# Thirty heads of a decode step as ten turns of a hardware loop, with each head's weights stored behind its keys

## The chip, the cores and the metric

The kernel runs on one core of one Trainium2 chip. The core has five engines with an instruction stream each: TensorE (PE, matmul), VectorE (DVE), ScalarE (ACT), GpSimd (POOL) and SyncE (SP); here SP issues nearly all DMA transfers. They meet only through semaphores. The metric is device time of one execution in microseconds (us), from the start to the end of the program. Lower is better.

## The reference

One token goes through a transformer block: attention over a cache of 8192 positions in 32 heads of 192 channels, then a squared-ReLU feed-forward network, both with a layer norm that is scaled and shifted by a condition `c`. All data is float32. The caches are 201 MB each, 403 MB together, and each number in them is used once.

```python
mod = (_silu(c) @ w_mod).reshape(c.shape[0], 6, 1, -1)
sa, ca, ga, sb, cb, gb = (mod[:, i] for i in range(6))
h = _layernorm(x) * (1 + ca) + sa
q = (h @ wq).reshape(1, 1, 32, 192).transpose(0, 2, 1, 3)
scores = einsum("bhqd,bhkd->bhqk", q, k_cache) * 192 ** -0.5
o = einsum("bhqk,bhkd->bhqd", softmax(scores), v_cache)
x = x + ga * (o.transpose(0, 2, 1, 3).reshape(1, 1, 32 * 192) @ wo)
h = _layernorm(x) * (1 + cb) + sb
r = relu(h @ w1 + b1)
x = x + gb * ((r * r) @ w2 + b2)
```

## The kernel before

The cache of a head is laid out as 128 partitions of 64 positions, so a head's keys are one tile of 128 x 12288 numbers (6144 KB), and its values are another. Three such tiles fit in on-chip memory: the pool `strm` hands out three slots in turn (`slot`, L47). The stream of loads is k0, v0, k1, v1 and so on, and load n takes the slot that load n-3 had. All of it is issued by SP in program order (`load`, L148). A load of keys so waits until the values of two heads earlier in the stream have been used by TensorE; a load of values waits until VectorE and ScalarE have finished with the keys of the head before.

For each head (loop at L257, unrolled by Python, so that the built program holds 32 copies of the body):

- `keys` (L183): VectorE multiplies the keys by the query in four chunks of 16 positions (L190) and sums most of the products of a chunk (L192). ScalarE sums the other 23 of a partition's 64 positions (L195).
- `softmax` (L208): the maximum over a partition (L210), over all partitions by a matmul (L212) and VectorE (L214), then the exponential on ScalarE (L218) and its sum by a matmul with ones (`total`, L88). The reciprocal of that sum (`inverse`, L206) is done in the middle of the next head.
- `values` (L222): 32 matmuls in four column groups multiply probabilities and values into `ps_o` (L229). The profile shows each float32 matmul as two.

Heads are paired for the weights. `load_w` (L136) fetches wo of pair i and wq of pair i+1 as one transfer of 1920 KB for two heads, into tiles of their own. In the third chunk of a head `between` runs either `project` (L232) for the pair that is finished, where VectorE scales two heads' outputs (L236), TensorE turns them (L241), VectorE copies (L244) and TensorE multiplies by wo (L248); or `query` (L172), which makes the queries of the next pair on TensorE (L176) and ScalarE (L178). Even heads from 2 on carry the projection, odd heads the query.

Ahead of the heads stand the matmuls for the condition (`mod`, L121) and the first layer norm. Behind them come the projection of the last pair, the second layer norm and the feed-forward network; its weights `w1` and `gw2` go into the slots that come free (L277 to L284). The order of the work is the order in which it is written (`manual_schedule`, L45); semaphores are placed by the language where data or buffers need them.

Of the kernel before, what the change touches and what calls it, by code (L numbers as in the profile page):

```python
# [8 lines left out]
F32 = mybir.dt.float32  # L9
AF = mybir.ActivationFunctionType  # L10
# [3 lines left out]
P = 128  # L14
D = 640
# [10 lines left out]
NPAIR = H // 2  # L26
NPOS = SK // P
I = 16
NCH = NPOS // I
N_ACT = (7, 6, 6, 4)  # L30
TAIL_PARTS = 4
WO = 3 * D
WQ = KB * PW
W2_CUT = ((0, 6), (6, 5), (11, 1))
EPS = 1e-5


@with_exitstack
def block_kernel(ctx: ExitStack, tc: tile.TileContext, xc, kc, vc, wq0, wx, wo15, wm0, wm1, w1, gw2, bb, out):
    nc = tc.nc  # L40
    const = ctx.enter_context(tc.tile_pool(name="const", bufs=1))
    strm = ctx.enter_context(tc.tile_pool(name="strm", bufs=3))
    work = ctx.enter_context(tc.tile_pool(name="work", bufs=2))
# [3 lines left out]
    def slot(name):  # L47
        return strm.tile([P, NPOS * DH], F32, tag="slot", name=name, bufs=3)

# [3 lines left out]
    ones = const.tile([P, P], F32, name="ones")  # L53
    nc.vector.memset(ones, 1.0)

# [14 lines left out]

    def columns(src, n, name, pool=const, **how):

        t = pool.tile([P, n // 32, 32], F32, name=name, **how)
        nc.vector.transpose(t.rearrange("p b r -> p (b r)"), src)
        return t
# [9 lines left out]
    def total(src, name):  # L85

        ps = psum.tile([P, 512], F32, tag="sm", name="ps_" + name, bufs=2)
        nc.tensor.matmul(ps[:, :1], ones, src, start=True, stop=True)  # L88
        return ps[:, :1]

    def layernorm(x, copies, scale1, shift, name):
# [5 lines left out]
        nc.vector.tensor_scalar(m, total(s, name + "_tm"), 1.0 / (copies * D), None, op0=ALU.mult)  # L97
# [6 lines left out]
        nc.scalar.activation(sd, total(ss, name + "_tv"), AF.Sqrt, bias=eps_t, scale=1.0 / (copies * D))  # L104
# [16 lines left out]
    def mod(first, n, w):  # L121

        ps = psum.tile([P, 512], F32, tag="q", name=f"ps_mod{first}", bufs=2)
        for b in range(KB):
            wb = w[:, b].rearrange("p (m n) -> p m n", m=n)
            for g in range(G):
                nc.tensor.matmul(ps[32 * g:32 * (g + 1), :n * DG], e[:, b:b + 1].to_broadcast([P, 32]),  # L127
                                 wb[:, :, DG * g:DG * (g + 1)], start=(b == 0), stop=(b == KB - 1))
        nc.vector.tensor_copy(mods[:, first:first + n], ps[:, :n * DG].rearrange("p (m n) -> p m n", m=n))  # L129

    wm0_t = slot("wm0_t")
    nc.sync.dma_start(wm0_t[:, :KB * 2 * D], wm0)

    qb_t, w_t = {}, {}

    def load_w(i):  # L136

        w_t[i] = strm.tile([P, WO + WQ], F32, tag="w", name=f"w{i}", bufs=2)
        if i < 0:
            nc.sync.dma_start(w_t[i][:, WO:], wq0)  # L140
        elif i + 1 == NPAIR:
            nc.sync.dma_start(w_t[i][:, :WO], wo15)
        else:
            nc.sync.dma_start(w_t[i], wx[i])

    k_t, v_t = {}, {}

    def load(src, to, h, what):  # L148
        to[h] = slot(f"{what}{h}")
        n = TAIL_PARTS if h == H - 1 and what == "v" else 1  # L150
        w = NPOS * DH // n
        for c in range(n):
            nc.sync.dma_start(to[h][:, c * w:(c + 1) * w],
                              src[h].rearrange("(p i) d -> p (i d)", p=P)[:, c * w:(c + 1) * w])

    load_w(-1)
    wm1_t = slot("wm1_t")
    nc.sync.dma_start(wm1_t[:, :KB * 3 * D], wm1)
    load(kc, k_t, 0, "k")
    mod(0, 2, wm0_t[:, :KB * 2 * D].rearrange("p (b n) -> p b n", b=KB))  # L160
# [11 lines left out]
    def query(i):  # L172
        w = w_t[i - 1][:, WO:].rearrange("p (b n) -> p b n", b=KB)
        ps = psum.tile([P, 512], F32, tag="q", name=f"ps_q{i}", bufs=2)
        for b in range(KB):
            nc.tensor.matmul(ps[:, :PW], hR[:, b], w[:, b], start=(b == 0), stop=(b == KB - 1))  # L176
        qb_t[i] = work.tile([P, PW], F32, name=f"qb{i}", tag="qb")
        nc.scalar.activation(qb_t[i], ps[:, :PW], AF.Copy, scale=DH ** -0.5)  # L178

    att = psum.tile([P, 512], F32, tag="att", name="att")  # L180
    query(0)

    def keys(h, between):  # L183

        q = qb_t[h // 2][:, DH * (h % 2):DH * (h % 2 + 1)]
        sc = work.tile([P, NPOS], F32, tag="sc", name=f"sc{h}")
        t = k_t.pop(h).rearrange("p (i d) -> p i d", d=DH)
        for c in range(NCH):
# [4 lines left out]
            for i in range(n, I):  # L193
                jk = work.tile([P, DH], F32, tag="jk", name=f"jk{h}_{c}_{i}", bufs=2)
# [5 lines left out]
        return sc  # L200

    ri_t, ps_t, sum_t = {}, {}, {}

    def inverse(h):
        ri_t[h] = work.tile([P, 1], F32, tag="ri", name=f"ri{h}", bufs=3)
        nc.vector.reciprocal(ri_t[h], sum_t.pop(h))  # L206

    def softmax(h, sc):  # L208
        mp = work.tile([P, 1], F32, tag="mp", name=f"mp{h}")
        nc.vector.tensor_reduce(mp, sc, axis=AX.X, op=ALU.max)  # L210
        ps = psum.tile([P, 512], F32, tag="sm", name=f"ps_mx{h}", bufs=2)
        nc.tensor.matmul(ps[:, :P], mp.to_broadcast([P, P]), ident, start=True, stop=True)  # L212
        nm = work.tile([P, 1], F32, tag="nm", name=f"nm{h}")
        nc.vector.tensor_reduce(nm, ps[:, :P], axis=AX.X, op=ALU.max, negate=True)  # L214

        p = work.tile([P, NPOS, 16], F32, tag="p", name=f"p{h}", bufs=1)
        sp = work.tile([P, 1], F32, tag="sp", name=f"sp{h}")
        nc.scalar.activation(p, sc[:, :, None].to_broadcast([P, NPOS, 16]), AF.Exp, bias=nm, accum_out=sp)  # L218
        sum_t[h] = total(sp, f"sum{h}")
        return p  # L220

    def values(h, p):  # L222

        t = v_t.pop(h)
        ps_t[h] = psum.tile([P, 512], F32, tag="o", name=f"ps_o{h}", bufs=3)
        n = NPOS // 2
        for j in range(n):
            g = j % G
            nc.tensor.matmul(ps_t[h][32 * g:32 * (g + 1), :PW], p[:, 2 * j:2 * j + 2].rearrange("p e r -> p (e r)"),  # L229
                             t[:, PW * j:PW * (j + 1)], start=(j < G), stop=(j >= n - G))  # L230

    def project(i):  # L232
        os_ = work.tile([P, 2, PW], F32, tag="os", name=f"os{i}", bufs=1)
        for a in range(2):
            h = 2 * i + a
            nc.vector.tensor_scalar(os_[:, :, DH * a:DH * (a + 1)], ps_t.pop(h)[:, :PW].rearrange("p (e d) -> p e d", e=2),  # L236
                                    ri_t.pop(h), None, op0=ALU.mult)
        pt = psum.tile([P, 512], F32, tag="sm", name=f"ps_oT{i}", bufs=2)
        for j in range(3):
            for k in range(2):  # L240
                nc.tensor.matmul(pt[:, 32 * j:32 * (j + 1)], os_[:, k, P * j:P * (j + 1)], pick[:, k],  # L241
                                 start=(k == 0), stop=(k == 1))
        oT = work.tile([P, 96], F32, tag="oT", name=f"oT{i}")
        nc.vector.tensor_copy(oT, pt[:, :96])  # L244
        w = w_t.pop(i)[:, :WO].rearrange("p (j n) -> p j n", j=3)
        for j in range(3):
            for g in range(G):
                nc.tensor.matmul(att[32 * g:32 * (g + 1), :DG], oT[:, 32 * j:32 * (j + 1)],  # L248
                                 w[:, j, DG * g:DG * (g + 1)],
                                 start=(i == 0 and j == 0), stop=(i == NPAIR - 1 and j == 2))  # L250

    mod(2, 3, wm1_t[:, :KB * 3 * D].rearrange("p (b n) -> p b n", b=KB))
    cb1 = const.tile([P, DG], F32, name="cb1")
    nc.vector.tensor_scalar(cb1, mods[:, 4], 1.0, None, op0=ALU.add)
    x_t = spread(x_c, KB, "x_t")
    bbt = spread(bbc, FB + KB, "bbt")
    for h in range(H):  # L257
        i = h // 2
        if h and h < H - 1:
            load(kc, k_t, h, "k")  # L260
        if h == H - 2:
            load(kc, k_t, h + 1, "k")
        if h % 2 and h < H - 1 or h == H - 2:
            load_w(i)
        load(vc, v_t, h, "v")

        def between():
            if h % 2 == 0 and h:
                project(i - 1)
            elif h % 2 and i + 1 < NPAIR:  # L270
                query(i + 1)

        sc = keys(h, between)
        values(h, softmax(h, sc))


    w1_t = slot("w1_t")  # L277
    nc.sync.dma_start(w1_t[:, :KB * FF], w1)
    gw_t = slot("gw_t")
    a = 0  # L280
    for b0, n in W2_CUT:
        b = KB * D + (b0 + n) * D
        nc.sync.dma_start(gw_t[:, a:b], gw2[:, a:b])
        a = b  # L284
# [77 lines left out]
```

## Time and profile before

| what | value |
|---|---|
| two timed runs | 1074.88 and 1075.42 us, median 1075.15 us |
| profiled execution, span | 1072.6 us |
| instructions | 8839 |
| TensorE busy | 431.8 us (40%) |
| VectorE busy | 756.2 us (70%) |
| ScalarE busy | 320.1 us (30%) |
| read from memory | 451.82 MB, 421 GB/s over the span |
| packets of SP's DMA queue | 98.1% of 16 engines' span |

The span goes from the first to the last instruction of the program in the profiled execution. The profile states no other time for that execution; the two timed runs lie 2.3 and 2.8 us above its span. In the views of the profile a row begins with the line of the kernel and the engine (PEld is TensorE's weight load, SPq the part of SP that issues), then the operation and the tiles as output<-input. "Idle before" is how long the engine had nothing to do ahead of a group of instructions, with what ended it.

### The profile page before, as it was taken

How to read it: one execution, taken by the hardware profiler on the slowest of the kernel's cores; microseconds unless marked ns; L12 is line 12 of the kernel's file. 1: busy time of each engine (PE TensorE's matmuls, PEld its weight loads, DVE VectorE, ACT ScalarE, POOL GpSimd, SP SyncE). 2: the span in 40 equal slices, each digit the busy share in tenths (PEclk: the TensorE clock that was granted, in tenths of full speed). 3: DMA queues.
4: the chain of work that ended last, by engine and by line, in shares of the span. 5: the costliest groups of instructions: out<-in, count | busy, mean ns of one | idle time of the engine just before them, and what ended most of it. 6: DMA issues, size and time to landing. Idle time of an engine off the chain costs nothing.

```text
span 1072.6 us, 8839 instructions
## 1 busy us (share of the span) xinstructions
PE 431.8 (40%) x3176; PEld 205.0 (19%) x3176; DVE 756.2 (70%) x453; ACT 320.1 (30%) x1559; POOL 0.7 (0%) x6
## 2 busy tenths in 40 slices
PE   3243243435425353442436344242633434363246
PEld 1011121113112121211113122111312111131113
DVE  1675877858578685858868586885757778585872
ACT  1132332323233232323422233332322323232340
POOL 0000000000000000000000000000000000000000
PEclk8666566666656666575666656566665666666568
DMA  9999999999999999999999999999999999999976
GB/s 401 438 426 435 419 442 436 428 431 433 428 422 442 424 439 424 437 429 427 435 437 424 440 424 438 425 432 432 426 436 423 430 435 426 433 428 426 399 292 266
DMA packets 13299, 452.38 MB, mean 422 GB/s; under 512 B 1732, under 2 KB 1736, under 8 KB 2120
## 3 DMA queue, kind: packets, MB, share of 16 engines
q1 hardware_dynamic: 12968, 451.81, 98.1%
q8 instruction: 25, 0.41, 0.2%
q14 instruction: 18, 0.15, 0.0%
q10 hardware_dynamic: 288, 0.01, 0.0%
HBM read 451.82 MB, written 0.00 MB: 421 GB/s over the span
## 4 chain that ended last, share of the span: by engine, by line
DMA 41%; DVE 38%; PE 18%; ACT 2%; issue 1%; SPq 0%; DVEq 0%; ACTq 0%
DMA k<-in_kc 41%; DVE k L190 21%; DVE sc L192 14%; PE ps_o L229 11%; PE ps_oT L241 4%; ACT p L218 2%; PE ps_mx L212 1%; PE ps_sum L88 1%; DVE os L236 1%; DVE nm L214 0%; PE ps_f L299 0%; DVE oT L244 0%; DVE mp L210 0%; PE ps_y L315 0%; ACT L218 0%
## 5 line engine op out<-in xcount | busy, mean ns | idle before, releaser
L190 DVE TENSOR_TENSOR k<-k,qb 128x3072 f32<-128x3072 f32 x128 | 428.5, 3348 | 192.9 <-DMA k<-in_kc 192.9
L195 ACT ACTIVATE jk<-k 128x192 f32<-128x192 f32 x736 | 256.5, 349 | 614.5 <-DVE k L190 614.5
L192 DVE TENSOR_REDUCE sc<-k 128x10 f32<-128x1920 f32 (+2 forms) x128 | 282.0, 2203 | 4.4
L229 PE MATMUL ps_o<-v,p 128*32 128x384 f32 x2048 | 240.0, 638 | 2.2 <-DMA v<-in_vc 2.2
L241 PE MATMUL ps_oT<-pick,os 128*128 128x32 f32 x192 | 43.2, 395 | 266.1 <-DVE os L236 266.1
L212 PE MATMUL ps_mx<-ident,mp 128*128 128x128 f32 x64 | 25.4, 501 | 285.6 <-DVE mp L210 285.6
L195 ACT ACTIVATION_READ_ACCUMULATOR jk<-k 128x1 f32 x736 | 137.3, 186 | 0.0
L229 PEld LDWEIGHTS ps_o<-v,p 128*32 128x32 f32 x2048 | 75.6, 140 | 144.9 <-issue 142.2
L241 PEld LDWEIGHTS ps_oT<-pick,os 128*128 128x128 f32 x192 | 41.0, 321 | 277.3 <-DVE os L236 276.6
L212 PEld LDWEIGHTS ps_mx<-ident,mp 128*128 128x128 f32 x64 | 16.1, 311 | 304.8 <-DVE mp L210 273.7
L218 ACT ACTIVATE p<-sc,nm 128x1024 f32<-128x1024 f32 x32 | 36.7, 1147 | 80.9 <-DVE nm L214 80.8
L176 PE MATMUL ps_q<-w,hR 128*128 128x384 f32 x150 | 52.4, 496 | 0.1
L88 PE MATMUL ps_sum<-sp,ones 128*128 128x1 f32 x64 | 18.8, 363 | 56.5 <-ACT p L218 56.5
L176 PEld LDWEIGHTS ps_q<-w,hR 128*128 128x128 f32 x150 | 27.3, 190 | 25.5 <-issue 8.8
L248 PE MATMUL att<-w,oT 128*32 128x160 f32 x384 | 28.5, 464 | 5.6 <-DVE oT L244 5.6
L244 DVE COPY oT<-ps_oT 128x96 f32<-128x96 f32 x16 | 4.1, 258 | 36.2 <-PE ps_oT L241 36.2
L214 DVE TENSOR_REDUCE nm<-ps_mx 128x1 f32<-128x128 f32 x32 | 9.3, 292 | 28.5 <-PE ps_mx L212 28.5
L88 PEld LDWEIGHTS ps_sum<-sp,ones 128*128 128x128 f32 x64 | 16.1, 313 | 65.9 <-ACT p L218 65.9
L236 DVE TENSOR_SCALAR os<-ps_o,ri 128x384 f32<-128x384 f32 x32 | 18.2, 607 | 7.3 <-PE ps_o L229 7.3
L248 PEld LDWEIGHTS att<-w,oT 128*32 128x32 f32 x384 | 15.6, 162 | 11.9 <-DVE oT L244 7.7
L127 PE MATMUL ps_mod<-wm_t,silu 128*32 128x320 f32 (+1 forms) x80 | 9.3, 626 | 12.5 <-DVE silu L117 12.5
L129 DVE COPY mods<-ps_mod 128x320 f32<-128x320 f32 (+2 forms) x3 | 1.4, 479 | 15.4 <-PE ps_mod L127 15.4
(68 smaller groups left out, 76.5 us busy)
## 6 DMA issues: line engine op xcount, KB each, us to landing
k<-in_kc SPq DMA_DIRECT2D x32, 6144.0 KB, 29.0
v<-in_vc SPq DMA_DIRECT2D x31, 6144.0 KB, 25.7
w<-in_wx SPq DMA_DIRECT2D x15, 1920.0 KB, 34.3
v<-in_vc SPq DMA_DIRECT2D x4, 1536.0 KB, 15.8
wm_t<-in_wm SPq DMA_DIRECT2D x1, 4800.0 KB
w_t<-in_w SPq DMA_DIRECT2D x1, 3840.0 KB, 12.6
gw_t<-in_gw SPq DMA_DIRECT2D x1, 3520.0 KB, 20.5
wm_t<-in_wm SPq DMA_DIRECT2D x1, 3200.0 KB, 10.7
```

The costliest lines, as they stand in the source:

```text
L88: nc.tensor.matmul(ps[:, :1], ones, src, start=True, stop=True)
L127: nc.tensor.matmul(ps[32 * g:32 * (g + 1), :n * DG], e[:, b:b + 1].to_broadcast([P, 32]), wb[:, :, DG * g:DG * (g + 1)], start=(b == 0), s ...
L176: nc.tensor.matmul(ps[:, :PW], hR[:, b], w[:, b], start=(b == 0), stop=(b == KB - 1))
L190: nc.vector.tensor_mul(pr, pr, q[:, None, :].to_broadcast([P, I, DH]))
L192: nc.vector.tensor_reduce(sc[:, c * I:c * I + n], pr[:, :n], axis=AX.X, op=ALU.add)
L195: nc.scalar.activation(jk, pr[:, i], AF.Copy, accum_out=sc[:, c * I + i:c * I + i + 1])
L212: nc.tensor.matmul(ps[:, :P], mp.to_broadcast([P, P]), ident, start=True, stop=True)
L218: nc.scalar.activation(p, sc[:, :, None].to_broadcast([P, NPOS, 16]), AF.Exp, bias=nm, accum_out=sp)
L229: nc.tensor.matmul(ps_t[h][32 * g:32 * (g + 1), :PW], p[:, 2 * j:2 * j + 2].rearrange("p e r -> p (e r)"), t[:, PW * j:PW * (j + 1)], star ...
L236: nc.vector.tensor_scalar(os_[:, :, DH * a:DH * (a + 1)], ps_t.pop(h)[:, :PW].rearrange("p (e d) -> p e d", e=2), ri_t.pop(h), None, op0=A ...
L241: nc.tensor.matmul(pt[:, 32 * j:32 * (j + 1)], os_[:, k, P * j:P * (j + 1)], pick[:, k], start=(k == 0), stop=(k == 1))
L248: nc.tensor.matmul(att[32 * g:32 * (g + 1), :DG], oT[:, 32 * j:32 * (j + 1)], w[:, j, DG * g:DG * (g + 1)], start=(i == 0 and j == 0), sto ...
```

## The change

Heads 1 to 30 become a loop that the chip runs: `tc.For_i(1, 31, 3, iteration_sync="staggered")`, ten turns with three heads in the body. Heads 0 and 31 stand outside. The loop needs fixed buffers: three tiles `slot0` to `slot2`, three queries `qb`, three PSUM tiles `ps_o` and three reciprocals are allocated once, and the address of a load in memory comes from the loop's counter. The slots rotate as before.

All weights of a head now lie in memory behind its keys: a row of `kx` holds 12288 numbers of keys, 960 of wq for the next head and 960 of wo for the head before, 7104 KB for a head in one transfer. `project` and `query` work on one head each and both run in each head's third chunk. The reciprocal follows the sum at once, so on VectorE it stands ahead of the next head's keys. The weights for the last five vectors of the condition are loaded at the end (`wm1`, 6880 KB with wo of head 31), and the keys of head 31 come in two parts.

```diff
-    for h in range(H):
...
+    head(0, 0, 1, lambda: query(1, slots[0][:, KV:KV + HW]))
+
+    with tc.For_i(1, H - 1, NH, iteration_sync=SYNC) as i:
+        for r0 in range(NH):
+            r = (r0 + 1) % NH
+            ks, vs = (2 * r0 + 2) % 3, (2 * r0 + 3) % 3
+            load_k(i + r0, ks)
+            load_v(i + r0, vs)
+
+            def between():
+                project((r - 1) % NH, slots[ks][:, KV + HW:])
+                query((r + 1) % NH, slots[ks][:, KV:KV + HW])
+
+            head(r, ks, vs, between)
+
+    r = (H - 1) % NH
+    ks, vs = 2, 0
+    half = KV // 2
+    nc.sync.dma_start(slots[ks][:, :half], kx[H - 1, :, :half])
+    nc.sync.dma_start(slots[ks][:, half:KV + HW], kx[H - 1, :, half:KV + HW])
+    load_v(H - 1, vs)
+    head(r, ks, vs, lambda: project((r - 1) % NH, slots[ks][:, KV:KV + HW]))
+
+    M = KB * 4 * D
+    nc.sync.dma_start(slots[1][:, :M + HW], wm1)
...
+    def load_k(h, s):
+        nc.sync.dma_start(slots[s], kx[bass.ds(h, 1)].rearrange("o p n -> (o p) n"))
...
+    def project(r, w, last=False):
+        os_ = work.tile([P, 2, DH], F32, tag="os", name="os_", bufs=2)
+        nc.vector.tensor_scalar(os_, ps_o[r][:, :PW].rearrange("p (e d) -> p e d", e=2), rs_[r], None, op0=ALU.mult)
+        for k in range(2):
+            nc.tensor.matmul(ps_t[:, :32], os_[:, k, :P], pick[:, k], start=(k == 0), stop=(k == 1))
+        for k in range(2):
+            for a in range(2):
+                nc.tensor.matmul(ps_t[64 * a:64 * (a + 1), 32:64], os_[:, k, P:], pick[:, k],
+                                 start=(k == 0), stop=(k == 1))
...
-            if c == 0 and h:
-                inverse(h - 1)
...
+        nc.vector.reciprocal(rs_[r], total(sp))
```

The loop's semaphores have to be set back in each turn. With the staggered form the body is cut into four stages, 0 to 3, with a counter each (`sem_stage_0` to `sem_stage_3`). Each of the five engines counts itself in when it enters a stage. At the entry to a stage it first waits for its own results of two stages before, counts itself out of that stage, and then waits until that stage's counter is below one, which means that all five have counted themselves out. The entry to stage 0 stands at the turn's end, and there each engine counts itself out of stage 2.

On SP, this is how the loads of heads 1 to 3 stood before, with the semaphores that each waits for (DMAHW are landings of transfers; `_49` marks counters of the whole program):

```order
L153 DMA k2_412<-in_kc 128x12288 [waits DMAHW6_49,DMAHW2_49,PE_49]
L153 DMA v2_414<-in_vc 128x12288 [waits DMAHW3_49,DMAHW7_49,DVE_49,Activation_49]
L153 DMA k3_541<-in_kc 128x12288 [waits DMAHW1_49,PE_49]
L144 DMA w1_543<-in_wx 128x3840
L153 DMA v3_545<-in_vc 128x12288 [waits DMAHW2_49,DVE_49,Activation_49]
L153 DMA k4_656<-in_kc 128x12288 [waits DMAHW3_49,PE_49]
```

And this is the rest of a turn on SP now, from its third load on (`ISA` computes an address; `_stg0` marks counters that are set back in the loop):

```order
L137 DMA slot1_67<-in_kx 128x14208 [waits DMAHW4_49,PE_49]
L140 ISA [waits sem_stage_3_1186]
L140 DMA slot2_68<-in_vc 128x12288 [waits DMAHW0_I-283_stg0,DVE_I-283_stg0,Activation_I-283_stg0]
L137 ISA
L137 DMA slot0_66<-in_kx 128x14208 [waits PE_I-283_stg1,DMAHW1_I-283_stg0]
L140 ISA [waits DMAHW0_I-283_stg0,DMAHW1_I-283_stg0,DMAHW2_I-283_stg0,sem_stage_0_1183]
L140 DMA slot1_67<-in_vc 128x12288 [waits DVE_I-283_stg2,Activation_I-283_stg2,Activation_I-283_stg1]
L226 REGISTER_ALU [waits DMAHW1_I-283_stg1,DMAHW0_I-283_stg1,sem_stage_1_1184,DMAHW0_I-283_stg2]
L226 COMPARE_AND_BRANCH
L226 UNCONDITIONAL_BRANCH [waits sem_stage_2_1185]
```

Before, each load waited for the users of its slot and nothing else. Now the six loads of a turn keep those waits, three of the four stage entries stand between them or behind the last, and SP meets the turn's end (the landing of its last load, `DMAHW0_I-283_stg2`, and the counter of stage 2) before it can issue the first load of the next turn.

TensorE counts itself out of stage 2 behind the last matmul of the turn. This is the end of a turn on TensorE:

```order
L163 MATMUL ps_q_95<-slot0_66,hR_160 128x192 x5
L208 MATMUL ps_m_97<-ident_69,mp_622 128x128
L96 MATMUL ps_m_97<-sp_628,ones_74 128x1
L221 MATMUL ps_o0_99<-slot1_67,p_627 32x384 x32
L226 REGISTER_ALU
L226 COMPARE_AND_BRANCH
```

There was no such place before: TensorE went from the values of one head straight on to the next head's query or projection. Ahead of the loop's first turn and behind its last stands a barrier of all five engines.

On VectorE, this is the border between two heads before, from the last chunk of head 2 to the first of head 3:

```order
L236 TENSOR_SCALAR os0_463<-ps_o0_264,ri0_320 128x2x192
L236 TENSOR_SCALAR os0_463<-ps_o1_379,ri1_433 128x2x192
L244 COPY oT0_473<-ps_oT0_466 128x96
L190 TENSOR_TENSOR k2_412<-k2_412,qb1_356 128x3072
L192 TENSOR_REDUCE sc2_416<-k2_412 128x12
L210 TENSOR_REDUCE mp2_497<-sc2_416 128x1
L214 TENSOR_REDUCE nm2_501<-ps_mx2_499 128x1
L190 TENSOR_TENSOR k3_541<-k3_541,qb1_356 128x3072
L192 TENSOR_REDUCE sc3_547<-k3_541 128x9
L206 RECIPROCAL ri2_564<-ps_sum2_506 128x1
```

And this is the same border now, between the first and the second head of a turn:

```order
L174 TENSOR_SCALAR os__342<-ps_o0_99,rsum0_105 128x384
L182 COPY oT_350<-ps_t_96 128x64
L198 TENSOR_TENSOR slot2_68<-slot2_68,qb1_103 128x3072
L200 TENSOR_REDUCE sc_297<-slot2_68 128x12
L207 TENSOR_REDUCE mp_376<-sc_297 128x1
L210 TENSOR_REDUCE nm_379<-ps_m_97 128x1
L215 RECIPROCAL rsum1_106<-ps_m_97 128x1
L198 TENSOR_TENSOR slot1_67<-slot1_67,qb2_104 128x3072
```

Each head now has one scaling and one copy where every second head had two and one, and the reciprocal has moved ahead of the next head's first product.

More of the change, by code (lines that the diff above doesn't have):

```diff
@@ L69, in block_kernel @@
     nc.scalar.dma_start(bbc, bb)
+    ps_q = psum.tile([P, 512], F32, name="ps_q")
+    ps_t = psum.tile([P, 512], F32, name="ps_t")
+    ps_m = psum.tile([P, 512], F32, name="ps_m")
+    att = psum.tile([P, 512], F32, name="att")
+    ps_o = [psum.tile([P, 512], F32, name=f"ps_o{i}") for i in range(NH)]
+    qb = [const.tile([P, DH], F32, name=f"qb{i}") for i in range(NH)]
+    rs_ = [const.tile([P, 1], F32, name=f"rsum{i}") for i in range(NH)]
     def columns(src, n, name, pool=const, **how):
@@ L83, in spread, with total @@
         return r
[L85 to L89, printed above, removed]
+    def total(src):
+        nc.tensor.matmul(ps_m[:, 256:257], ones[:, :P], src, start=True, stop=True)
+        return ps_m[:, 256:257]
     def layernorm(x, copies, scale1, shift, name):
@@ L180, in block_kernel @@
[L180 to L187, printed above, removed]
+            nc.tensor.matmul(ps_q[:, :DH], hR[:, b], w[:, b], start=(b == 0), stop=(b == KB - 1))
+        nc.scalar.activation(qb[to], ps_q[:, :DH], AF.Copy, scale=DH ** -0.5)
+    query(0, slots[2][:, KB * 2 * D:KB * 2 * D + HW])
@@ L188, in keys, with head @@
+    def head(r, ks, vs, between, inverse=True):
+        q = qb[r]
+        sc = work.tile([P, NPOS], F32, tag="sc", name="sc", bufs=2)
+        t = slots[ks][:, :KV].rearrange("p (i d) -> p i d", d=DH)
         for c in range(NCH):
@@ L228, in values @@
             g = j % G
[L229 to L250, printed above, removed]
```

207 lines of the change are left out of this document (89 added, 118 removed).

## The prediction

> **What bounds the kernel now.** First the page's rows on the DMA queues, then time slices by stretch of the program (start and end of the stretch and its length; busy time of PE, PEld, DVE, ACT and POOL; granted clock; DMA share; GB/s).
>
> ```profile
> DMA  9999999999999999999999999999999999999976
> q1 hardware_dynamic: 12968, 451.81, 98.1%
> ...
> 228.40:959.00 730.60, 291.99 (x2070) 139.87 (x2074) 537.95 (x291) 226.13 (x1118) 0.00 (x0) 0.63 1.00 431
> 959.00:1020.00 61.00, 22.18 (x162) 11.00 (x154) 45.81 (x25) 19.14 (x95) 0.00 (x0) 0.64 0.98 418
> 1020.00:1040.00 20.00, 7.58 (x66) 2.67 (x66) 18.90 (x10) 8.39 (x46) 0.00 (x0) 0.67 0.64 265
> ```
>
> The DMA engines are full at 431 GB/s until near the end; VectorE is busy 537.95 of 730.6 us in the same stretch. Bytes set the time, and anything that leaves the queue empty is paid in full. Then the sizes of the transfers, the waits of VectorE, and the waits of SP's queue.
>
> ```profile
> k<-in_kc SPq DMA_DIRECT2D x32, 6144.0 KB, 29.0
> v<-in_vc SPq DMA_DIRECT2D x31, 6144.0 KB, 25.7
> w<-in_wx SPq DMA_DIRECT2D x15, 1920.0 KB, 34.3
> ...
> DVE k L190 <- DMA k<-in_kc: 192.9, 31, 10.8
> ...
> SPq L153 <- DVE sc L192: 633.9, 31, 28.9
> SPq L153 <- PE ps_o L229: 316.3, 30, 12.0
> ```
>
> A tile of 6144 KB is 6.291 MB, 14.6 us at 431 GB/s. Keys land 29.0 and values 25.7 us after issue, so a load is queued 11 to 14 us before its predecessor is through. That lead, earned by freeing one slot at a time, keeps the queue full. SP waits only for slots, VectorE for keys (192.9 us, 31 times).
>
> The last view is the order of time over one head with a projection (start, length, engine; rows of ScalarE's sums left out), with the load that its values release.
>
> ```profile
> 924.67 0.33 SPq L153 DMA_DIRECT2D k<-in_kc  x1
> 925.96 3.36 DVE L190 TENSOR_TENSOR k<-k,qb 128x3072 f32<-128x3072 f32 x1 [10.69 <-DMA k<-in_kc]
> 942.20 1.13 DVE L236 TENSOR_SCALAR os<-ps_o,ri 128x384 f32<-128x384 f32 x2
> 942.86 2.77 PE L241 MATMUL ps_oT<-pick,os 128*128 128x32 f32 x12 [18.26 <-DVE os L236]
> 945.98 1.83 PE L248 MATMUL att<-w,oT 128*32 128x160 f32 x24 [0.35 <-DVE oT L244]
> 949.22 2.55 DVE L192 TENSOR_REDUCE sc<-k 128x12 f32<-128x2304 f32 x1
> 951.84 0.33 SPq L153 DMA_DIRECT2D v<-in_vc  x1
> 952.99 0.29 DVE L214 TENSOR_REDUCE nm<-ps_mx 128x1 f32<-128x128 f32 x1 [0.89 <-PE ps_mx L212]
> 953.37 1.15 ACT L218 ACTIVATE p<-sc,nm 128x1024 f32<-128x1024 f32 x1 [2.60 <-DVE nm L214]
> 955.18 7.20 PE L229 MATMUL ps_o<-v,p 128*32 128x384 f32 x64
> ...
> 962.45 0.33 SPq L153 DMA_DIRECT2D k<-in_kc  x1
> ```
>
> With its keys landed at T = 925.96, VectorE ends at T+25.8, the exponential starts at T+27.4, the values run from T+29.2 to T+36.4 (962.38), and SP issues the next keys 0.07 us later. The head's own values need only 14.6 us of DMA behind its keys. So TensorE ends a head about 22 us after its last byte, and before the change the queue works on later heads in that time.
>
> **The change, part by part.** *Bytes.* Unchanged: 441,216 KB on both sides by the loads in the code, 451.8 MB. I keep 431 GB/s for rows of 56,832 bytes, since rows of 49,152 and the smaller ones of `w` ran in one stretch at that mean. A head's keys with weights take 7104 KB, 16.9 us; a head 31.5 us, as before in the mean.
>
> *The turn's end.* SP may issue the first keys of a turn only when all five engines have counted themselves out of stage 2, and TensorE does that behind the last values matmul of the turn. Until now that load needed only the values of the head before to be used. What hides behind nothing any more is the tail of one head per turn. What is late next: the keys of the next turn, with 16.9 us of landing, and then all that hangs on them.
>
> *A head's own tail* changes little. VectorE scales one head where it scaled two (1.13 us x2 above, so 0.57 us less); the reciprocal (one small instruction, under 0.2 us) goes behind the softmax, where VectorE waits for keys anyway; TensorE's turning keeps 12 rows, 8 of them with half the weights. Against that, `query` now stands in the same chunk, and ScalarE must do the query's copy before its last four sums. Its matmuls are priced by the row
>
> ```profile
> 899.89 3.49 PE L176 MATMUL ps_q<-w,hR 128*128 128x384 f32 x10
> ```
>
> as 3 to 3.5 us behind the projection's. From scaling at T+16.2: turning to T+19, wo to T+20.6, query to T+23.8, then five ScalarE instructions of about 0.35 us: T+25.6, where VectorE ends at T+25.1. So this is about even with T+25.8, and I keep T+36.3 for the end of the values, 35 to 38 as bounds.
>
> *From TensorE to data.* SP's reaction was 0.07 us; a few semaphore and address instructions come in between, for which no row exists: 0.1 to 3 us (SP's dearest issue row is below 1 us), I take 0.6. From issue to data stand these slices at the program's start, where SP issued at 0.74 us:
>
> ```profile
> 0.74 0.39 SPq L132 DMA_DIRECT2D wm_t<-in_wm  x1
> ...
> 0.70:1.70 1.00, 0.00 (x0) 0.00 (x0) 0.72 (x11) 0.04 (x1) 0.50 (x2) 1.00 0.00 0
> 1.70:2.70 1.00, 0.00 (x0) 0.00 (x0) 0.09 (x2) 1.00 (x1) 0.00 (x0) 1.00 1.60 410
> ```
>
> That is 1.0 us. Together 1.6.
>
> *When TensorE counts itself out.* Its counting instruction stands behind 64 matmul rows that take 7.20 us. No row shows whether the instruction stream runs ahead of the array. If not, it comes at T+36.3; at the earliest when the other engines are there, which is ScalarE behind the maximum, T+27.4, 8.9 us sooner. I take 3 us sooner, nearer the first end, since the semaphore that SP waited for until now came with the matmuls' end. The Trainium skill ("TensorE: Matmul & The Clock Gate", table at the top) gives TensorE a queue of 64 instructions, and "Perfetto Trace Analysis" (Sequencer Loop) has the sequencer push an instruction and go on. By that the count comes when half of the 128 loads and matmuls are still queued, which by the row of 7.20 us would be an estimate of 3.6 us early and 1286 us in all; no row of this trace shows it.
>
> *The sum of a turn.* From the first data of its first keys: 16.9 us plus 0.5 to T of the first head; two heads of 31.5 us to T of the third; 36.3 to its last matmul; less 3; plus 1.6. That is 17.4 + 63.0 + 36.3 - 3 + 1.6 = 115.3 us, where three heads of bytes need 94.5: 20.8 us of empty queue per turn, ten times 208 us. Within a turn the values of the second head are now issued only after stage 1 is open, at T+27.4 of the first instead of at T+25.8. With T at 17.4 that is 44.8 from first data, and the queue holds work until 16.9 + 14.6 + 16.9 = 48.4: 3.6 us of cover, 1.0 of it for issue. If the first head were over 2.6 us longer, each turn would lose the excess. The other stage entries stand where all engines have long been.
>
> *Entry.* The barrier ahead of the loop keeps SP from issuing keys 1 until head 0 is through.
>
> ```profile
> 21.27 0.82 DVE L170 COPY hR<-ln_h 128x640 f32<-128x640 f32 x1
> 22.14 5.92 PE L176 MATMUL ps_q<-w-1_101,hR 128*128 128x384 f32 x10 [1.93 <-DVE hR L170]
> 39.89 3.36 DVE L190 TENSOR_TENSOR k<-k,qb 128x3072 f32<-128x3072 f32 x1 [4.51 <-DMA k<-in_kc]
> ...
> 891.61 3.36 DVE L190 TENSOR_TENSOR k<-k,qb 128x3072 f32<-128x3072 f32 x1 [1.71 <-DMA k<-in_kc]
> ...
> 917.18 7.42 PE L229 MATMUL ps_o<-v,p 128*32 128x384 f32 x64
> ```
>
> Keys 0 now come behind 3680 KB instead of 8960 KB: 39.89 less 12.5 is 27.4, I take 28; their query, half as wide, is done before. A head without a projection runs from 891.61 to 924.60, 33 us. So 28 + 33 - 3 + 1.6 + 0.5 for the barrier: data of turn 1 starts at 60.
>
> *Tail.* Ten turns end at 60 + 1153 = 1213 and the barrier behind the loop at 1213.5. From there keys 31, values 31 and `wm1` (6624 + 6144 + 6880 KB) take 46.7 us, `mod` with its copies about 6 us, and the rest is the chain from the last scaling to the end of the span:
>
> ```profile
> 1050.33 0.62 DVE L236 TENSOR_SCALAR os<-ps_o,ri 128x384 f32<-128x384 f32 x1 [7.35 <-PE ps_o L229]
> 1058.51 4.80 PE L299 MATMUL ps_f<-w_t,hT 128*32 128x384 f32 x40 [1.71 <-DVE hT L74]
> 1065.69 3.47 PE L315 MATMUL ps_y<-gw_t,fT 128*32 128x160 f32 x96 [1.02 <-DVE fT L74]
> 1069.92 0.66 SPq L320 DMA_DIRECT2D out_y<-y  x1
> ```
>
> 22.3 us to 1072.6. `w1` and `w2` (7680 KB, 18.2 us) land at 64.9 behind the loop, before the chain needs the last of them at about 68. So 46.7 + 0.6 + 6 + 22.3 = 75.6, and the span ends at 1213.5 + 75.6 = 1289. Crosscheck: 1072.6 + 208 + 18 for the entry (42 to 60), less the 7 us that the queue now loses at 1020 to 1040 (0.64 of 20 us busy), is 1292. The profiled execution's span is 2.55 us below the median of the two runs, and the profile gives no other time for it; with that, 1289 + 2.5 + 1, between the two sums, is **1293 us**.
>
> **The rivals.** *One head's tail is not waited for, only the last landing.* If the counts came so early that just SP's own wait at the turn's end remained (the landing of the last values), each of the nine borders within the loop would cost 0.5 + 1.6 = 2.1 us, while the two barriers still cost 18 each: 1072.6 + 19 + 36 - 7 + 2.5 = 1123. For it: staged counters are there to let engines differ by a stage. Against it: TensorE's count stands behind the matmuls which themselves wait for that landing and for the exponential.
>
> *Not slower.* The same mechanism at all eleven seams, barriers included: engines count themselves out of a stage as soon as their instructions are queued, and no seam costs more than the drained queue, 2.1 us. Then 1072.6 + 23 - 7 + 2.5 = 1091, within 2%. It decides where a seam costs less than (21.5 + 7) / 11 = 2.6 us, 21.5 us being 2%, which is about what a measurement of this kernel can tell from no change. Against it: a VectorE that ends at T+25.8 and an exponential at T+27.4 cannot be counted out earlier by any view above, and the last byte is there at T+14.
>
> *Dearer seams.* The jump back makes engines fetch instructions, which the page's rows of before do not price on SP. The Trainium skill ("Runtime: NRT & Kernel Launch", Instruction fetch mechanics) says that a taken branch to a place outside the two blocks of instructions that an engine holds forces a fetch before execution goes on. As a mechanism here: on the other engines 17 us of landing cover it; on SP it would lengthen each seam, by 3 us at my upper bound, and if the first head also outruns its 2.6 us of cover by 2 us, 1293 + 26 + 20 = 1339. It stays in the range.
>
> **How the numbers follow.** The forecast, a tail of one head per seam, has 0.80; only the last landing 0.07; not slower 0.06; dearer than the range 0.07. The range takes the bounds of the unknowns: TensorE's count 3 us later at eleven seams, +33, and SP's 2 us more, +22, give 1348; the count 5.9 us sooner, -65, gives 1228. Both ends at once are unlikely, so 1235 to 1345 for 8 in 10. Slower by over 2% is the forecast, the dear end and 1123: 0.94. Within 2% I give 0.04 and faster 0.02, out of the not-slower case.
>
> **What would show it.** DMA slices with 20 us of nothing once per 115 us, ten times, and a first one near 42 us; SP's first key load of a turn released by TensorE's last values, the other two key loads as before; VectorE idle about 23 us before the first keys of a turn (17.4 + 36.3 - 3 + 1.6 less its own 29); span near 1290 with unchanged busy times of VectorE and ScalarE. Gaps of 2 us would show the first rival. Gaps over 25 us would show an unpriced step at the seam, more than one gap per turn the cover of 2.6 us gone. A DMA rate off 431 GB/s between gaps would make the bytes' term wrong.

## The result, and the profile after

The changed kernel takes 1319.16 us (median of 1318.72 and 1319.60) against 1075.15: a ratio of 1.2274, 95% interval 1.2238 to 1.2309. The forecast of 1293 us had the sign and the place right and was 26 us short. The profiled execution spans 1314.6 us, 242 us more than before.

From the page of the changed kernel, the slices of DMA, SP's queue, the dearest group, and the two large kinds of loads:

```profile
DMA  9399849949993995799399669939975993998495
q1 hardware_dynamic: 10376, 451.81, 80.1%
L198 DVE TENSOR_TENSOR slot<-slot,qb 128x3072 f32<-128x3072 f32 x128 | 428.9, 3351 | 322.7 <-DMA slot<-in_kx 322.7
...
slot<-in_kx SPq DMA_DIRECT2D x30, 7104.0 KB, 26.2
slot<-in_vc SPq DMA_DIRECT2D x32, 6144.0 KB, 20.5
```

The bytes are the same, 451.81 MB. The row of nines has become a row with a hole every three to four slices, and VectorE waits 322.7 us for keys where it waited 192.9, though its busy work per chunk is unchanged (428.9 us for the products, 3351 ns each).

The holes, with what stands between them, by stretches of time (columns as before: PE, PEld, DVE, ACT, POOL busy, clock, DMA share, GB/s):

```profile
42.80:64.20 21.40, 8.25 (x68) 3.27 (x68) 10.28 (x7) 6.41 (x24) 0.00 (x0) 0.58 0.00 1
64.20:161.30 97.10, 31.04 (x216) 16.48 (x212) 60.83 (x32) 24.39 (x124) 0.00 (x0) 0.61 0.98 419
...
417.70:513.60 95.90, 31.53 (x220) 16.26 (x212) 60.87 (x32) 24.41 (x125) 0.00 (x0) 0.63 0.99 424
513.60:534.50 20.90, 13.93 (x102) 7.60 (x106) 9.33 (x8) 5.12 (x23) 0.00 (x0) 0.64 0.00 0
...
1213.60:1234.80 21.20, 14.12 (x106) 7.45 (x106) 9.40 (x9) 5.13 (x23) 0.00 (x0) 0.65 0.00 0
```

For 21 to 23 us no data moves, while TensorE and VectorE finish a head. There are eleven such holes: one at the entry, and one at each of the ten turn ends, of 21.0 to 22.7 us, 215 us together. Inside a turn the queue is never empty. The entry's hole is 21.9 us long, from 42.8 to the keys' first data at 64.65 (what moves at 64.20 is 8 KB of instructions). That makes 237 us of the 242.

One turn's way to the next, in order of time (start, length, engine, line):

```profile
416.80 0.33 SPq L137 DMA_DIRECT2D slot<-in_kx  x1
436.41 3.36 DVE L198 TENSOR_TENSOR slot<-slot,qb 128x3072 f32<-128x3072 f32 x1 [26.08 <-DMA slot<-in_kx]
467.73 3.36 DVE L198 TENSOR_TENSOR slot<-slot,qb 128x3072 f32<-128x3072 f32 x1 [2.40 <-DMA slot<-in_kx]
496.47 7.71 PE L221 MATMUL ps_o<-slot,p 128*32 128x384 f32 x64
499.43 3.36 DVE L198 TENSOR_TENSOR slot<-slot,qb 128x3072 f32<-128x3072 f32 x1 [2.68 <-DMA slot<-in_kx]
527.50 7.56 PE L221 MATMUL ps_o<-slot,p 128*32 128x384 f32 x64
533.55 0.33 SPq L137 DMA_DIRECT2D slot<-in_kx  x1
```

The last bytes of this turn landed at 513.6. VectorE works on the third head's keys, the softmax follows, the values run to 535.06 (527.50 + 7.56), and SP issues the next keys 1.51 us before that end. The slot of those keys had been free since the second head's values matmuls ended at 504.18, 29 us before.

What SP waited for stands in the trace too, in the semaphore instructions, which the views leave out. At this turn's end SP had counted itself out at 513.96, ScalarE at 525.76 and VectorE at 527.64. TensorE's count, the last, ended at 533.02, which is 2.04 us ahead of the end of its last matmul. The other engines went on at 533.05 and 533.06, and SP's issue followed 0.50 us behind that. At all nine turn ends within the loop TensorE is the last, 2.0 us ahead of its last matmul's end, and SP needs 0.5 us.

### The profile page after: what moved, and what is told of

It reads as the page before. It is cut to its first block, busy times and chain, and to the rows that moved or that the text cites. A ratio compares the mean times of both kernels' runs of the same rounds, so it can differ in the third digit from the quotient of the medians.

```text
span 1314.6 us, 10909 instructions
## 1 busy us (share of the span) xinstructions
PE 506.7 (39%) x3704; PEld 267.3 (20%) x3704; DVE 762.6 (58%) x470; ACT 320.9 (24%) x1575; POOL 0.7 (0%) x6
## 3 DMA queue, kind: packets, MB, share of 16 engines
q1 hardware_dynamic: 10376, 451.81, 80.1%
## 4 chain that ended last, share of the span: by engine, by line
DMA 39%; DVE 24%; PE 24%; issue 7%; ACT 2%; SPq 0%; ACTq 0%; DVEq 0%
DMA slot<-in_kx 35%; DVE slot L198 15%; PE ps_o L221 11%; DVE sc L200 6%; PE ps_q L163 5%; DMA slot<-in_wm 4%; PE ps_t L176 2%; PE att L184 1%; ACT jk L203 1%; PE att L188 1%; PE ps_t L179 1%; PE ps_m L96 1%; PE ps_m L208 1%; PE ps_q L133 1%; DVE os__342 L174 0%
## 5 line engine op out<-in xcount | busy, mean ns | idle before, releaser
L198 DVE TENSOR_TENSOR slot<-slot,qb 128x3072 f32<-128x3072 f32 x128 | 428.9, 3351 | 322.7 <-DMA slot<-in_kx 322.7
L203 ACT ACTIVATE jk<-slot 128x192 f32<-128x192 f32 x736 | 256.1, 350 | 662.4 <-DVE slot L198 659.1
L200 DVE TENSOR_REDUCE sc<-slot 128x10 f32<-128x1920 f32 (+2 forms) x128 | 282.0, 2203 | 4.4
L221 PE MATMUL ps_o<-slot,p 128*32 128x384 f32 x2048 | 243.5, 646 | 0.0
L176 PE MATMUL ps_t<-pick,os__342 128*128 128x32 f32 x40 | 10.6, 406 | 350.5 <-DVE os__342 L174 350.5
L203 ACT ACTIVATION_READ_ACCUMULATOR jk<-slot 128x1 f32 x736 | 137.8, 187 | 0.0
L221 PEld LDWEIGHTS ps_o<-slot,p 128*32 128x32 f32 x2048 | 76.3, 141 | 145.4 <-issue 144.9
L163 PE MATMUL ps_q<-slot,hR 128*128 128x192 f32 x320 | 102.5, 499 | 2.4 <-DVE hR L158 1.9
L163 PEld LDWEIGHTS ps_q<-slot,hR 128*128 128x128 f32 x320 | 90.5, 309 | 17.7 <-issue 14.7
L176 PE MATMUL ps_t<-pick,os__465 128*128 128x32 f32 x40 | 10.6, 406 | 119.8 <-DVE os__465 L174 119.8
L176 PE MATMUL ps_t<-pick,os__588 128*128 128x32 f32 x40 | 10.6, 406 | 119.5 <-DVE os__588 L174 119.5
L184 PE MATMUL att<-slot,oT 128*32 128x160 f32 x256 | 28.4, 466 | 12.2 <-DVE oT L182 12.2
```

Source lines behind the costliest of these rows:

```text
L163: nc.tensor.matmul(ps_q[:, :DH], hR[:, b], w[:, b], start=(b == 0), stop=(b == KB - 1))
L176: nc.tensor.matmul(ps_t[:, :32], os_[:, k, :P], pick[:, k], start=(k == 0), stop=(k == 1))
L184: nc.tensor.matmul(att[32 * g:32 * (g + 1), :DG], oT[:, :32], w[:, DG * g:DG * (g + 1)], start=False, stop=False)
L198: nc.vector.tensor_mul(pr, pr, q[:, None, :].to_broadcast([P, I, DH]))
L200: nc.vector.tensor_reduce(sc[:, c * I:c * I + n], pr[:, :n], axis=AX.X, op=ALU.add)
L221: nc.tensor.matmul(ps_o[r][32 * g:32 * (g + 1), :PW], p[:, 2 * j:2 * j + 2].rearrange("p e r -> p (e r)"), v[:, PW * j:PW * (j + 1)], star ...
```

## The experiments

**The loop alone.** Heads 1 to 30 are unrolled by Python; layout, buffers and per-head work stay those of the changed kernel.

```diff
-    with tc.For_i(1, H - 1, NH, iteration_sync=SYNC) as i:
+    for i in range(1, H - 1, NH):
```

> The loop is written out by Python, all else as changed: weights behind the keys, projection and query in every head, the new tail. If the seams of the loop hold all of the loss (ten at the turns' ends and one at the entry, 21.5 us each in the trace), the queue has no gap and the time is 1068 to 1083 us: 1319 less 236, with the rest of a turn at 94.3 to 95.6 us for three heads. If larger rows, or projection and query in every head, cost part of it, the time stays above 1100 us.

It took 1069.63 us, ratio to before 0.9957 (0.9943 to 0.9971). Its slices, its queue, and the stretch in which the kernel before had lost 7 us:

```profile
DMA  9999999999999999999999999999999999999994
q1 hardware_dynamic: 10376, 451.81, 98.4%
...
1020.00:1040.00 20.00, 12.15 (x104) 5.46 (x108) 7.74 (x8) 4.64 (x15) 0.00 (x0) 0.60 0.99 427
```

No hole is left. So the loop costs all of it, and the other half of the change (weights behind the keys, queries per head, reciprocal at once) costs nothing: the share of 0.64 at 1020 to 1040 us has become 0.99, and this version is 0.4% shorter than before, a small difference that its interval sets apart from none.

**Five turns of six heads** instead of ten of three.

```diff
-    with tc.For_i(1, H - 1, NH, iteration_sync=SYNC) as i:
-        for r0 in range(NH):
+    with tc.For_i(1, H - 1, 2 * NH, iteration_sync=SYNC) as i:
+        for r0 in range(2 * NH):
```

> Six heads in a turn, five turns instead of ten. If each turn's end costs one gap of 21.5 us whatever the turn holds, five gaps go: 1319 - 107 = 1212 us, 1205 to 1220. If the loss is per head (transfers, projection, query), nothing changes: 1319.

It took 1231.01 us (like all numbers below that have no interval, one run), above the range. The five turn ends cost 21.0 to 22.4 us each, as they should. But each turn has a new hole in its middle, of 3.2 to 4.7 us, 19.5 together, which is the miss. One of them, and the load that ends it:

```profile
397.30:400.40 3.10, 3.10 (x40) 1.06 (x36) 1.03 (x1) 0.00 (x0) 0.00 (x0) 0.92 0.00 0
...
399.51 0.33 SPq L140 DMA_DIRECT2D slot<-in_vc  x1
```

TensorE is busy throughout, with values matmuls. With six heads the automatic cut put TensorE's entry to stage 2 behind 29 of a head's 32 values matmuls, and SP's entry to that stage stands ahead of this load. TensorE's count ends at 399.13, the last of the five, and SP issues 0.38 us later. So it is not only the turn's end that can hold SP; any entry can.

**A plain barrier at the turn's end** instead of the staggered form.

```diff
-SYNC = "staggered"
+SYNC = "barrier"
```

> The staggered reset is replaced by the plain barrier at the turn's end. If the staggered form already acts as a meeting of all engines at the turn's end, only the cost of the barrier is added, 1 to 4 us a turn: 1329 to 1360 us. If staggering still hides a good part of a head's tail, the gaps grow by more than 5 us each: above 1370 us.

It took 1315.99 us, less than expected and within 0.3% of the changed kernel. A turn end, and the place of the entry's hole:

```profile
495.20:519.30 24.10, 14.91 (x106) 7.89 (x106) 9.42 (x9) 5.14 (x23) 0.00 (x0) 0.68 0.00 0
...
42.80:64.00 21.20, 8.28 (x68) 3.26 (x68) 14.11 (x9) 7.30 (x29) 0.00 (x0) 0.59 1.01 434
...
509.24 7.76 PE L221 MATMUL ps_o<-slot,p 128*32 128x384 f32 x64
...
518.37 0.33 SPq L137 DMA_DIRECT2D slot<-in_kx  x1
```

SP issues 1.37 us behind the last matmul (517.00) instead of 1.5 ahead of it, and nine turn ends lose 2.5 us more (24.06 instead of 21.52 in the mean). But the first turn has no hole: this form has no barrier ahead of the loop that SP must pass, and the first keys, issued at 27.35, are already moving at 42.8. What had been left out of the expectation is that entry. The two effects nearly cancel (spans of 1314.2 and 1314.6 us), so here the staggered form earns nothing that one run could show.

**The same turns, ending elsewhere.** Each head's values move into the next head's part, so that a turn ends behind a softmax, and each load is written where its slot comes free. Ten turns, three heads and the staggered form remain.

```diff
-            ks, vs = (2 * r0 + 2) % 3, (2 * r0 + 3) % 3
-            load_k(i + r0, ks)
-            load_v(i + r0, vs)
+            ks, free = (2 * r0 + 2) % 3, (2 * r0 + 1) % 3
+            values((r - 1) % NH, free)
+            load_k(i + (r0 + 1), free)
...
-            head(r, ks, vs, between)
+            keys(r, ks, between, lambda: load_v(i + (r0 + 1), ks))
```

> Same loop, same ten turns, same stage counters; the turn is cut elsewhere. The values of a head move into the next head's part, so a turn ends behind a softmax, and the loads are written where their slots come free: the next head's keys behind the values, the next head's values behind the keys. At the turn's end the next keys are in flight and the next values are queued. If what costs is that the loads stand behind TensorE's count at the turn's end, the gaps go: 1075 to 1090 us. If the jump itself is dear (fetching instructions, setting semaphores back), the loss stays by its share: at 20 us a turn about 1290 us, at 3 us about 1110.

It took 1129.15 us, ratio 1.0502 (1.0485 to 1.0520): 190 of the 244 us back, yet outside the range. The holes of 21 us are gone, also the entry's. Ten of 2.65 to 5.08 us are left, one per turn:

```profile
522.60:527.70 5.10, 5.10 (x44) 1.63 (x40) 1.01 (x1) 0.00 (x0) 0.00 (x0) 0.61 0.07 19
...
513.91 2.55 DVE L203 TENSOR_REDUCE sc<-slot 128x12 f32<-128x2304 f32 x1
...
520.89 8.18 PE L225 MATMUL ps_o<-slot,p 128*32 128x384 f32 x64
...
526.72 0.33 SPq L140 DMA_DIRECT2D slot<-in_vc  x1
```

The load at 526.72 is one of values, into a slot whose keys VectorE had summed by 516.5 and ScalarE by 517.4. But the automatic cut had put TensorE's entry to stage 3 behind 31 of the 32 values matmuls of this run (520.89 to 529.07), and SP's entry to that stage ahead of this load. TensorE's count ends at 526.36, and SP issues 0.36 us later. It is the mechanism of the turn's end in small.

**The cuts placed by hand.** The skewed loop again, with the three inner cuts behind the softmax of the turn's first and second head and, in the third, behind the projection and the query, where no values matmuls stand ahead that SP must wait for.

```diff
                 project((r - 1) % NH, slots[ks][:, KV + HW:])
                 query((r + 1) % NH, slots[ks][:, KV:KV + HW])
+                if r0 == 2:
+                    tc.stage_boundary()
 
             keys(r, ks, between, lambda: load_v(i + (r0 + 1), ks))
+            if r0 < 2:
+                tc.stage_boundary()
```

> The skewed loop, with the three cuts between its stages put by hand: behind the softmax of the turn's first and second head and, in the third head, behind the projection of the head before, so that no entry stands behind values matmuls that SP's next load waits for. Theory of the meeting points: the ten gaps of 2.65 to 5.08 us that the skewed loop had left (together about 40 us) go, and the time falls from 1129 to about 1086 us (1073 to 1095). Rival, a turn of a loop costs some 3 to 5 us for itself, wherever its stages are cut: 1129 us (1120 to 1135). In no case below 1068, what the unrolled program took less its rounding, since the bytes are the same.

It took 1086.49 us, ratio 1.0113 (1.0096 to 1.0130), where about 1086 was expected.

```profile
DMA  9999999999999999999999999999999999999993
...
434.71 3.36 DVE L201 TENSOR_TENSOR slot<-slot,qb 128x3072 f32<-128x3072 f32 x1 [4.71 <-issue]
440.81 0.33 SPq L140 DMA_DIRECT2D slot<-in_vc  x1
...
436.00:446.00 10.00, 2.59 (x12) 1.46 (x16) 6.30 (x6) 2.73 (x10) 0.00 (x0) 0.55 0.88 339
467.00:477.00 10.00, 5.71 (x34) 3.13 (x37) 4.96 (x6) 2.94 (x11) 0.00 (x0) 0.67 0.99 430
```

Ten turns of a staggered loop thus end within 17 us of the unrolled program, and not 250 behind it. No hole of the kind above is left. What remains is one more meeting per turn, at the third cut: there VectorE stands idle for 4.7 to 5.3 us in each turn, until ScalarE, which waits for TensorE's query, has counted itself out (at 434.46 here). VectorE so ends the third head's keys late, and the values that take their slot are issued at 440.81, only 1.2 us before the keys ahead of them have landed; the next two heads' values are issued 4.6 us or more ahead. Around that handover 339 GB/s move, around another 430. The head with the late load takes 33.2 us of the queue in the mean instead of 31.3, and 1.9 us in each turn is about what remains. Another place for that cut was not tried.

**More matmuls at the turn's end, and at its start.** 32 further matmuls into a spare PSUM tile, once behind the last head's values, once behind the first head's. They are work that the reference has not.

```diff
+    hx = hR.rearrange("p b r -> p (b r)")
+
+    def idle_matmuls():
+        n = NPOS // 2
+        for j in range(n):
+            g = j % G
+            nc.tensor.matmul(ps_x[32 * g:32 * (g + 1), :PW], hx[:, 32 * g:32 * (g + 1)], hx[:, :PW],
+                             start=(j < G), stop=(j >= n - G))
...
             head(r, ks, vs, between)
+            if r0 == 2:
+                idle_matmuls()
```

The second run has `r0 == 0` in its place.

> Adds work that is not in the reference: 32 matmuls of the values' shape (128*32 by 128x384, operands from hR, result into a spare PSUM tile that nobody reads) behind the last head's values of each turn. Theory of the turn's end (SP's first keys of a turn wait until TensorE has worked through everything that stands behind the last values matmul): 32 such matmuls took 8.24 us in the changed kernel, so each of the ten gaps in the transfers grows from 21.5 us to about 29.7, the entry's stays at 21, and the time is 1319 + 82 = 1401 us (1390 to 1408). Rival, only the landing of the last transfer and the code of the next turn hold SP: gaps of 21.5 us as they were, 1319 us (1316 to 1325), since nothing reads the new tile and TensorE is busy for 507 of 1315 us.

> Adds the same 32 matmuls, which are not in the reference, but behind the values of the first head of each turn. Theory of the turn's end: TensorE does them while the later heads' bytes move, no stage entry that SP waits for at an empty queue stands behind them, and the time stays at 1319 us (1317 to 1327). Rival, TensorE's work costs time wherever it stands in a turn (a longer body, more code, a busier engine): as much as at the end, about 1400 us.

At the end: 1379.78 us, 60.6 more. Two turn ends, and the order of time at one:

```profile
409.80:436.00 26.20, 19.17 (x166) 9.70 (x170) 9.38 (x8) 5.12 (x23) 0.00 (x0) 0.71 0.00 0
533.00:559.00 26.00, 18.98 (x166) 9.45 (x170) 9.37 (x8) 5.13 (x23) 0.00 (x0) 0.71 0.00 0
...
423.85 7.60 PE L222 MATMUL ps_o<-slot,p 128*32 128x384 f32 x64
431.27 5.34 PE L231 MATMUL ps_x<-hR 128*32 128x384 f32 x64
...
435.10 0.33 SPq L138 DMA_DIRECT2D slot<-in_kx  x1
```

Nothing reads the new tile, but SP waits until TensorE has counted itself out behind it (at 434.57) and issues at 435.10, again 1.51 us before TensorE's last matmul ends (436.61). The ten holes average 26.4 us, 4.9 more than in the changed kernel, close to the 5.34 that the extra matmuls take. The landing rival (1319) is out. The expected 1401 was too high because 32 values matmuls had been taken as the price (8.24 us), and these are shorter because the granted clock was higher:

```profile
423.85:431.27 7.42, 7.42 (x65) 2.52 (x68) 0.17 (x1) 0.00 (x0) 0.00 (x0) 0.69 0.00 0
431.27:436.61 5.34, 5.34 (x68) 1.84 (x60) 0.00 (x0) 0.00 (x0) 0.00 (x0) 1.00 0.48 149
```

The rest, about 12 us, is not in the holes: SP's fourth load of a turn comes 49.0 us behind its first instead of 46.7, since the added instructions moved VectorE's entry to stage 1 behind the reciprocal.

At the start: 1363.97 us. The theory said 1319, so this was a miss; by the number alone the rival, that matmuls cost time wherever they stand, looked better. The trace says otherwise: the holes at the turn's ends are still 20.8 to 22.4 us, and time goes inside the turn.

```profile
309.20:408.90 99.70, 36.47 (x284) 21.93 (x276) 60.79 (x32) 24.38 (x124) 0.00 (x0) 0.65 0.97 408
...
373.66 2.15 DVE L201 TENSOR_REDUCE sc<-slot 128x10 f32<-128x1920 f32 x1
375.73 0.61 DVE L175 TENSOR_SCALAR os__498<-ps_o,rsum 128x384 f32<-128x384 f32 x1
...
375.18 0.33 SPq L138 DMA_DIRECT2D slot<-in_kx  x1
```

SP's fifth load, the third head's keys, comes 66.8 us behind the first (375.18 here, where the turn's first was issued at 308.26), and not 56.1 as in the changed kernel. The extra instructions had moved the automatic cut: SP's entry to stage 2 now stood ahead of the fifth load instead of the sixth, and VectorE's ahead of the scaling that starts at 375.73. VectorE counted itself out at 373.70 and ScalarE, the last, at 374.93, 0.25 us before SP's issue. So the experiment had changed two things.

**The same, with the cuts held.** The extra matmuls at the start again, with the cuts written out at the places where they had stood in the changed kernel (VectorE's entry to stage 2 stands one instruction earlier); the loads are called early enough to keep their stages. The first `cut` below is in `project`, which gets it for the turn's second head, the others in `head`.

```diff
+            if cut and g == 0:
+                tc.stage_boundary()
...
+            if cut == 2 and c == 2:
+                tc.stage_boundary()
...
+        if cut == 0:
+            tc.stage_boundary()
         nc.vector.reciprocal(rs_[r], total(sp))
...
-            load_k(i + r0, ks)
+            if r0 == 0:
+                load_k(i, ks)
             load_v(i + r0, vs)
+            if r0 < 2:
+                load_k(i + (r0 + 1), 1 - r0)
```

> The same 32 extra matmuls behind the values of each turn's first head (they are not in the reference), but with the three cuts between the stages written out at the places where they stood in the changed kernel, so that nothing but the matmuls differs. Theory of the moved cuts (the run before cost 4.4 us a turn because the extra instructions had moved the cut between the second and third stage, and SP's fifth load waited for VectorE there): the loads go back to their old times, the matmuls lie beside transfers, and the time is 1319 us (1315 to 1324). Rival, matmuls cost in the middle of a turn by themselves: 1364 us (1358 to 1370).

It took 1319.24 us, the changed kernel's time to 0.01%.

```profile
299.50:395.00 95.50, 35.29 (x284) 17.56 (x276) 60.84 (x31) 24.40 (x124) 0.00 (x0) 0.65 0.99 424
395.00:416.30 21.30, 14.17 (x102) 8.08 (x106) 9.45 (x9) 5.13 (x23) 0.00 (x0) 0.58 0.01 3
...
298.52 0.33 SPq L138 DMA_DIRECT2D slot<-in_kx  x1
...
354.70 0.33 SPq L138 DMA_DIRECT2D slot<-in_kx  x1
```

The fifth load is back at 56.2 us behind the first. 32 matmuls are free in the middle of a turn and cost 4.9 us at its end: what counts is only what stands between the last byte and the meeting of the engines.

## Why the prediction was right, and where it was short

**The mechanism held.** The signs that it named are there: an empty queue of about 20 us at each turn's end and one near 42 us, no other hole, SP's first key load of a turn released by TensorE's count behind the last values, and VectorE idle before the first keys of a turn, for 26.08 us in the row above where about 23 was put. The unrolled run shows that the seams are all of the loss, the matmuls at the end show that SP waits for TensorE's stream, and the skewed loop shows that it is the place of the meeting, not the number of turns.

**The term for a turn, 17.4 + 63.0 + 36.3 - 3 + 1.6 = 115.3 us, was 1.7 short; measured 117.0.** As means over the ten turns, modelled ends of matmuls included:

| term | predicted | measured |
|---|---|---|
| first data to first keys in use | 17.4 | 18.7 |
| first to third head's keys | 63.0 | 62.8 |
| third head's keys to the last values matmul | 36.3 | 36.1 |
| last matmul to next data | -1.4 | -0.5 |

Two terms were mis-sized. The keys were in use 1.3 us later than their bytes at 431 GB/s plus 0.5; in the row above, 436.41 less the data at 417.75, 18.7. The bytes had been divided by the rate of the whole queue, but the keys did not have the queue to themselves until their end: in every turn their last packet ended 18.0 to 18.6 us behind their first, while packets of the values behind them began at 17.3 to 17.6.

The other term is TensorE's count. It was taken 3 us before TensorE's end, and the trace has it at 2.0. SP's way from there to the issue was taken as 0.6 and took 0.5, and the 1.0 us from issue to data held (0.96). The Trainium skill ("TensorE: Matmul & The Clock Gate", table at the top) names a queue of 64 instructions, from which the prediction's estimate was 3.6 us. The trace does not bear that estimate out: the count came 2.0 us ahead, with 20 matmul rows and 16 weight loads still to start.

**The entry was 4.7 us short** (data at 64.65 instead of 60).

```profile
28.98 0.72 DVE L89 COPY bbt_c<-bbc 128x544 f32<-128x544 f32 x1 [4.27 <-DMA bbc<-in_bb]
30.40 3.32 DVE L198 TENSOR_TENSOR slot<-slot,qb 128x3072 f32<-128x3072 f32 x1
...
54.13 1.28 ACT L214 ACT_TABLE_LOAD   x1 [2.67 <-DVE nm L210]
...
57.23 7.17 PE L221 MATMUL ps_o<-slot,p 128*32 128x384 f32 x64
```

Keys 0 were expected in use at 28; the keys' last packet ended at 28.2, but VectorE began at 30.40, because a small transfer for the biases landed late too and VectorE had its copy ahead of the keys. Head 0 then took 34.0 us (30.40 to 64.40) and not 33; a table load of 1.28 us stands in its softmax. The rest, 1.2 us, lies between the head's last matmul and the data: 0.25 us passed there, where -3 + 1.6 + 0.5 had been put.

**The tail was 4.1 us short** (75.6 from the barrier, 79.7 from the first data behind it).

```profile
1284.03 7.04 PE L133 MATMUL ps_q<-slot,silu 128*32 128x480 f32 x40 [4.25 <-DMA slot<-in_wm]
...
1291.99 0.61 DVE L174 TENSOR_SCALAR os__811<-ps_o,rsum 128x384 f32<-128x384 f32 x1
```

The three loads took 49.2 us to 1284.03 where 46.7 + 0.6 was put; `mod` with its copies took 8.0 (to 1291.99) where about 6 was put; the chain to 1314.6 took 22.6 against 22.3. Entry, turns and tail make 4.7 + 17.2 + 4.1 = 26 us less the 0.5 for the barrier, which is in the tail's start. Outside the span lay 4.1 us where 2.5 was put, and the forecast stood 1 us above this sum, between its two.

**The cover held.** The second head's values came 46.7 us behind the turn's first issue, so their data about 46.8 us behind the first data, and by the bytes the queue held until 48.4: 1.6 of 2.6 us were left. The run with matmuls at the turn's start, whose fifth load came 10.7 us late, shows how that cover goes.

**The rivals.** "Only the last landing" and "not slower" fall with the unchanged 21 us and with the matmuls at the end. "Dearer seams" named instruction fetching on SP. No run shows it: SP had passed its branch at 514.13 in the turn above, 19 us before TensorE's count, and issued 0.5 us behind that count, with 5.34 us of additional matmuls as without. So a fetch, if there was one, lay inside that wait. The excess came from a landing and a count-out, both smaller than that rival's.

## What to carry to other kernels

Read a hardware loop's stage entries as meetings of all engines: the engine that feeds a full DMA queue must not meet, ahead of its next load, an engine that still has a tail of dependent work. Let a turn end where every engine is nearly level, write each load where its slot comes free, and place the inner cuts by hand; here that took the loop's cost from 250 us to 17. An edit that adds instructions to such a loop can move automatic cuts, so before an experiment on its body is believed, the cuts have to be held.

## What the runs showed that was not expected

- The staggered form was no better than a plain barrier here (1319.16 and 1315.99 us). It saves 2.5 us per turn, but its barrier ahead of the loop left the queue empty for 21.9 us.
- 32 matmuls of the same shape took 5.34 us with operands from `hR` and 7.60 us as values matmuls in the same turn. The granted clock was 0.50 up to 428.4, in the first part of the values matmuls, and 1.00 from there on; at 1.00 a matmul row took 0.49 us in both groups.
- The automatic cut can cost as much as real work: 44.7 us in ten turns (1363.97 against 1319.24 us), with the same work and the cuts elsewhere.
